# Two batches loaded as nine tokens per partition, both weights ahead of the second batch, and the min/add of two blocks on GpSimd

## The chip, the cores and the metric

The kernel runs on one core of a Trainium2 chip. The time is the device time of that core in microseconds (us). The programs have one core, so a run is called slow when it lies over 1.5% above the fastest run of the same kernel; verdicts use the other ("fast") runs. Every ratio below is the mean time of one kernel's fast runs over the mean time of the fast runs of the kernel before in the same rounds on the same chip, so it is not quite the ratio of the medians that are quoted beside it. One per cent is 4.0 us.

The engines are TensorE (PE in the profile; PEld is its weight load), VectorE (DVE), ScalarE (ACT), GpSimd (POOL), and SyncE (SP), which issues most DMAs. Each has its own queue of instructions.

## The reference, cut to what matters

```python
# per batch (8) and head (8), 576 tokens, 64 wide
out_d = softmax(mean4(q) @ mean4(k).T / 8) @ mean4(v)            # 144 pooled tokens
out_l = softmax(where(|i-j| < 4, q @ k.T / 8, -1e9)) @ v         # a band of 7
x = repeat4(out_d) + out_l                                       # 4608 x 512 in all
h = x @ w_in                                                     # 512 -> 2048
g = where(h > 0, h, exp(min(h, 0)) - 1)                          # ELU
y = g @ w_out                                                    # 2048 -> 512
```

The kernel handles heads in pairs, attention by batch (576 tokens), and the two products in 9 blocks of 512 tokens. "mm1" is x @ w_in, 16 pieces of 4 matmuls a block (tile hp); "mm2" is g @ w_out, 16 pieces as well (tile op).

## The kernel before: the parts that matter

The ELU is max(h,0) + (min(exp(h),1) - 1). In every block ScalarE makes the exp, and VectorE both following steps:

```python
def mm1(t, fc):
    tag = "misc" if t < 2 and fc % 2 else "hp"           # four banks in blocks 0 and 1, two later
    hp = ps.tile([128, TBLK], FP32, tag=tag, bufs=2, name="hp")
    # ... four matmuls into hp
    nc.scalar.activation(out=e[:], in_=hp[:], func=AF.Exp)
    nc.vector.tensor_scalar(                              # "the min/add"
        out=e[:], in0=e[:], scalar1=1.0, scalar2=-1.0, op0=AB.min, op1=AB.add)
    nc.vector.scalar_tensor_tensor(                       # frees the hp bank
        out=gts[t][:, fc, :], in0=hp[:], scalar=0.0, op0=AB.max, in1=e[:], op1=AB.add)
```

q, k and v come with one token per partition, so each run in memory is 64 floats, 256 B; GpSimd casts everything that is loaded (q, k, v, weights) to fp16 and adds the two attention outputs into x:

```python
nc.sync.dma_start(out=q32[:], in_=rows(q, 0, NB, 0, QB))   # [96 tokens][12 blocks][64]
# ... k and v with three DMAs each (edge rows)
nc.gpsimd.tensor_copy(out=q16[:], in_=q32[:].rearrange("p e c d -> p c e d"))   # k, v likewise
```

Weights are loaded in 16 pieces through three buffers, mixed into the loads of batch 1; the softmax denominators of a batch are 36 matmuls (288 or 144 columns).

The softmax here doesn't subtract the row's maximum and nothing guards it: scores larger than these inputs give would overflow.

Of the kernel before, what the change touches and what calls it, by code (L numbers as in the profile page):

```python
# [17 lines left out]
QB, KW, NB = 96, 102, 6  # L18
HB = 3 * QB
QW, KWW = QB + 24, 24 + KW  # L20
# [5 lines left out]
RW = S + SD  # L26
KG = SD // 2


def _np_consts():  # L30

    off = np.concatenate([np.arange(96), np.arange(-3, 0), np.arange(96, 99)])
    m = np.zeros((KW, NB, QB), dtype=np.float16)
    for c in range(NB):
        for u in range(QB):
            ok = (np.abs(off - u) < 4) & (off + QB * c >= 0) & (off + QB * c < S)
            m[ok, c, u] = 1.0
    r = np.zeros((KW, 24), dtype=np.float16)
    r[np.arange(96), np.arange(96) // 4] = 0.25
    qi = np.concatenate([np.eye(96, dtype=np.float16), r[:96]], axis=1)  # L40
    ki = np.concatenate([r, np.eye(KW, dtype=np.float16)], axis=1)
    vr = np.zeros((KW, 120), dtype=np.float16)
    vr[:, 48:72] = r
    indl = np.zeros((128, 37), dtype=np.float16)
    indl[:, 5] = 1.0
    seed = np.zeros((2, 32 + HB), dtype=np.float16)
    seed[0, 6:32] = 1.0
    seed[1, 4:6] = 1.0
    seed[0, 32:] = 1.0
    seed[1, 32 + SD :] = 1.0  # L50
    sel = np.zeros((NPAIR, 32, 3, 2, 64), dtype=np.float16)
    for e in range(2):
        for g in range(2):
            sel[:, 2 * e + g, g, e] = 1.0
        sel[:, 4 + e, 2, e] = 1.0
    return m, qi, ki, vr, indl, seed, sel.reshape(128, 384)
# [12 lines left out]
def kernel(  # L69
# [14 lines left out]

    def const(a, name):
        t = sb.tile(list(a.shape), FP16, tag=name, bufs=1, name=name)
        nc.sync.dma_start(out=t[:], in_=nc.inline_tensor(a, name=name + "c").ap())
        return t

    def two(name):  # L90
        return ps.tile([128, 2, 512], FP32, tag="two", bufs=2, name=name)

    m_np, qi_np, ki_np, vr_np, ind_np, seed_np, sel_np = _np_consts()
    QI, KI = const(qi_np, "QI"), const(ki_np, "KI")
    consts = {}

    def late_consts():
        consts["VR"] = const(vr_np, "VR")
        consts["MASK"] = const(m_np, "MASK")
        consts["IND"] = const(ind_np, "IND")  # L100
        consts["SEED"] = const(seed_np, "SEED")
        consts["SEL"] = const(sel_np, "SEL")
# [4 lines left out]
    def load_weights(i):  # L107

        w32 = sb.tile([128, 1024], FP32, tag="w32", bufs=3, name="w32")
# [9 lines left out]
        return lambda: nc.gpsimd.tensor_copy(out=to, in_=w3)  # L119


    st16, stT, stB, stS, stR = {}, {}, {}, {}, {}

    st32 = {}

    def load(b, j):
        q32 = sb.tile([QB, 2, NB, 64], FP32, tag="q32", bufs=3, name="q32")
        k32 = sb.tile([KW, 2, NB, 64], FP32, tag="k32", bufs=3, name="k32")
        v32 = sb.tile([KW, 2, NB, 64], FP32, tag="v32", bufs=3, name="v32")

        def rows(src, c0, nblk, tok, n):
            a = src[b, 2 * j]
            blocks = [[QB * D, 2 * NB]] if nblk == NB else [[S * D, 2], [QB * D, nblk]]
            return bass.AP(
                tensor=a.tensor, offset=a.offset + (QB * c0 + tok) * D,
                ap=[[D, n], *blocks, [1, D]],
            )

        nc.sync.dma_start(out=q32[:], in_=rows(q, 0, NB, 0, QB))
        for src, dst in ((k, k32), (v, v32)):  # L140
            nc.sync.dma_start(out=dst[0:96], in_=rows(src, 0, NB, 0, QB))
            lo = 1 if (b, j) == (0, 0) else 0
            hi = NB - 1 if (b, j) == (B - 1, NPAIR - 1) else NB
            if lo or hi < NB:
                nc.gpsimd.memset(dst[96:KW, :, 0 if lo else NB - 1, :], 0.0)
            for c0, nblk, tok, p in ((lo, NB - lo, -3, 96), (0, hi, QB, 99)):
                to, a = dst[p : p + 3, :, c0 : c0 + nblk, :], rows(src, c0, nblk, tok, 3)
                if nblk == NB:
                    nc.sync.dma_start(out=to, in_=a)  # L149
                else:  # L150
                    for e in range(2):
                        nc.sync.dma_start(out=to[:, e], in_=a[:, e])
        st32[(b, j)] = (q32, k32, v32)

    def cast(b, j):
        q32, k32, v32 = st32.pop((b, j))
        q16 = sb.tile([QB, NB, 2, 64], FP16, tag="q16", bufs=2, name="q16")
        k16 = sb.tile([KW, NB, 2, 64], FP16, tag="k16", bufs=2, name="k16")
        v16 = sb.tile([KW, NB, 2, 64], FP16, tag="v16", bufs=8, name="v16")
        nc.gpsimd.tensor_copy(out=q16[:], in_=q32[:].rearrange("p e c d -> p c e d"))  # L160
        nc.gpsimd.tensor_copy(out=k16[:], in_=k32[:].rearrange("p e c d -> p c e d"))
        nc.gpsimd.tensor_copy(out=v16[:], in_=v32[:].rearrange("p e c d -> p c e d"))
        st16[(b, j)] = (q16, k16, v16)


    def transposes(b, j):
        q16, k16, v16 = st16.pop((b, j))
        VR = consts["VR"]
        tq, tk = two("tq"), two("tk")
        for c in range(NB):  # L170
            nc.tensor.matmul(  # L171
                tq[:, c // 3, QW * (c % 3) : QW * (c % 3) + QW], q16[:, c, :, :], QI[:],
                start=True, stop=True,
            )
        for c in range(NB):
            nc.tensor.matmul(  # L176
                tq[0:KG, c // 3, 3 * QW : 3 * QW + 128],
                VR[:, 48 - 24 * (c % 3) : 120 - 24 * (c % 3)], v16[:, c, :, :],
                start=(c % 3 == 0), stop=(c % 3 == 2),
            )  # L180
        qt = sb.tile([128, 2, 3 * QW], FP16, tag="qt", bufs=2, name="qt")
        nc.scalar.copy(out=qt[:], in_=tq[:, :, 0 : 3 * QW])  # L182
        vd = sb.tile([KG, 2, 128], FP16, tag="vd", bufs=8, name="vd")
        nc.vector.tensor_copy(out=vd[:], in_=tq[0:KG, :, 3 * QW : 3 * QW + 128])  # L184
        for c in range(NB):
            nc.tensor.matmul(  # L186
                tk[:, c // 3, KWW * (c % 3) : KWW * (c % 3) + KWW], k16[:, c, :, :], KI[:],
                start=True, stop=True,
            )
        tk4 = tk[:, :, 0 : 3 * KWW].rearrange("p g (c w) -> p g c w", w=KWW)  # L190
        kt = sb.tile([128, 2, 3, KW], FP16, tag="kt", bufs=2, name="kt")
        nc.scalar.copy(out=kt[:], in_=tk4[:, :, :, 24:KWW])  # L192
        kd = sb.tile([128, 2, 3, 24], FP16, tag="kd", bufs=2, name="kd")
        nc.vector.tensor_copy(out=kd[:], in_=tk4[:, :, :, 0:24])  # L194
        stT[(b, j)] = (qt, kt, kd, vd, v16)


    def scores(b, j):
        qt, kt, kd, vd, v16 = stT.pop((b, j))
        sc = [two("sc"), two("sc")]  # L200
        for c in range(NB):
            for e in range(2):
# [3 lines left out]
                    kt[r, c // 3, c % 3, :],  # L206
                    qt[r, c // 3, QW * (c % 3) : QW * (c % 3) + QB],
                    start=True, stop=True,
                )
        for kg in range(2):  # L210
            for e in range(2):
                r = slice(64 * e, 64 * e + 64)
                qd = _free(qt[r, 0, QB : QB + 1], [[QW, NB], [1, 24]])
                nc.tensor.matmul(  # L214
                    sc[e][0:KG, kg, HB : HB + SD],
                    _free(kd[r, 0, 0, 0:1], [[1, SD]])[:, KG * kg : KG * kg + KG], qd,
                    start=True, stop=True,
                )
        pex = sb.tile([KW, 2, S], FP16, tag="pex", bufs=2, name="pex")
        dex = sb.tile([KG, 2, 2, SD], FP16, tag="dex", bufs=8, name="dex")  # L220
        for e in range(2):
            nc.scalar.activation(  # L222
                out=pex[:, e, :].rearrange("p (g u) -> p g u", g=2),
                in_=sc[e][0:KW, :, 0:HB], func=AF.Exp, scale=SCALE,
            )
            nc.scalar.activation(  # L226
                out=dex[:, e], in_=sc[e][0:KG, :, HB : HB + SD], func=AF.Exp, scale=SCALE,
            )
        mex = sb.tile([KW, 2, S], FP16, tag="mex", bufs=8, name="mex")
        mk = consts["MASK"][:].rearrange("p c u -> p (c u)")  # L230
        mk2 = bass.AP(tensor=mk.tensor, offset=mk.offset, ap=[list(mk.ap[0]), [0, 2], [1, S]])
        nc.vector.tensor_tensor(out=mex[:], in0=pex[:], in1=mk2, op=AB.mult)  # L232
        stS[(b, j)] = (mex, dex, vd, v16)


    def denominators(b):
        den = ps.tile([128, 512], FP32, tag="misc", bufs=2, name="den")
        SEED, IND = consts["SEED"], consts["IND"]
        for j in range(NPAIR):
            nc.tensor.matmul(  # L240
# [44 lines left out]
    def spread_pe(b, j0):  # L285

        rc, SEL = stR[b], consts["SEL"]
        if j0 == 0:
            stB[b] = sb.tile([128, NPAIR, RW], FP16, tag="rcb", bufs=2, name="rcb")
# [212 lines left out]
```

## Time and profile before

| | before |
|---|---|
| median of 2 runs | 402.4 us (401.56 to 403.25) |
| profiled span, mean granted TensorE clock | 401.8 us, 0.979 |
| TensorE busy | 353.0 us, so 48.8 us idle |
| VectorE, ScalarE, GpSimd busy | 254.4, 203.8, 138.7 us |

Three rows of the page's second part (the span in 40 slices of 10 us; the digits are tenths):

```profile
PE   1465688687986899999999999999899899999996
PEclk9999999968999799999999999999999999999999
GB/s 121 189 253 258 190 215 234 265 126 134 198 139 130 189 176 16 172 231 125 28 195 217 118 78 194 226 64 121 172 79 33 102 53 28 49 29 28 52 54 78
```

TensorE is nearly full from 160 us on. Before that it has holes, and the clock that the throttle grants is below 0.9 in three slices (digits 6, 8 and 7). The first slices move little, 121 and 189 GB/s. The same in the table by stage, for 0 to 10 us and for the stretches of block 0's and of block 1's mm1 (columns: stretch, its length, then busy us and instructions of each engine, granted clock, DMA share, GB/s):

```profile
0.00:10.00 10.00, 1.28 (x12) 1.16 (x13) 0.00 (x0) 1.28 (x1) 3.03 (x9) 1.00 0.67 120
...
45.00:72.00 27.00, 22.21 (x150) 10.80 (x149) 22.40 (x38) 15.03 (x29) 16.04 (x21) 1.00 1.12 224
...
108.00:143.00 35.00, 28.47 (x307) 16.07 (x305) 26.91 (x51) 21.75 (x42) 16.24 (x22) 0.90 0.84 158
```

Three milestones in TensorE's timeline (start, length, engine, line, operation, output<-input, shapes, count): mm1 of block 0, mm2 of block 0 and mm1 of block 1 begin here. Next come the denominators of a later batch, at full clock:

```profile
44.86 0.61 PE L368 MATMUL hp<-xt,WI 128*128 128x512 f16 x1
...
72.49 1.02 PE L388 MATMUL op<-WO,gt 128*128 128x512 f16 x4 [0.83 <-DVE gt L377]
...
108.07 1.03 PE L368 MATMUL hp<-xt,WI 128*128 128x512 f16 x4
...
306.08 0.30 PE L240 MATMUL den<-SEED 2*32 2x288 f16 x4
306.32 0.68 PE L248 MATMUL den<-mex,IND 102*32 102x288 f16 x16
306.82 0.42 PE L257 MATMUL den<-dex,IND 72*32 72x144 f16 x16
307.18 0.60 PE L388 MATMUL op<-WO,gt 128*128 128x512 f16 x2
```

And two groups of the page's fifth part (busy us, mean ns of one | idle time before them, and what ended it):

```profile
L377 DVE SCALAR_TENSOR_TENSOR gt<-hp,e 128x512 f16<-128x512 f32 x144 | 99.6, 692 | 5.4
L374 DVE TENSOR_SCALAR e<-e 128x512 f16<-128x512 f16 x144 | 63.8, 443 | 51.5 <-ACT e L373 50.5
```

The min/add takes 0.443 us on average, and VectorE's last step, 0.692 us, hardly ever waits.

### The profile page before, as it was taken

The numbers are of one execution on the slowest core, as the hardware profiler recorded it, in microseconds if no ns is written. First come the engines' busy times: TensorE is split into PE (matmuls) and PEld (weight loads), VectorE is DVE, ScalarE is ACT, GpSimd is POOL, SyncE is SP. The second block draws the span as 40 slices with busy tenths as digits, with TensorE's granted clock in tenths as the row PEclk, the third lists the DMA queues.
The fourth block names the chain that finished last, engine by engine and source line by source line (L and its number), as shares of the span: only waits on it lengthen the run. The fifth ranks groups of instructions, "written<-read, shape, count | busy, mean of one in ns | idle before, by whom it ended". The sixth has DMA issues, their size and how long they took to land.

```text
span 401.8 us, 8092 instructions
## 1 busy us (share of the span) xinstructions
PE 353.0 (88%) x3052; PEld 185.6 (46%) x3052; DVE 254.4 (63%) x460; ACT 203.8 (51%) x377; POOL 138.7 (35%) x184
## 2 busy tenths in 40 slices
PE   1465688687986899999999999999899899999996
PEld 1352345343553455555545554555454444444442
DVE  0134599732586797697778769886886585555510
ACT  1462157535385376747564855667375334444321
POOL 3365755460850581075028304820450050000000
PEclk9999999968999799999999999999999999999999
DMA  6998999965966980796199639926820310100112
GB/s 121 189 253 258 190 215 234 265 126 134 198 139 130 189 176 16 172 231 125 28 195 217 118 78 194 226 64 121 172 79 33 102 53 28 49 29 28 52 54 78
DMA packets 138082, 53.81 MB, mean 134 GB/s; under 512 B 122580, under 2 KB 131388, under 8 KB 138044
## 3 DMA queue, kind: packets, MB, share of 16 engines
q1 hardware_dynamic: 129420, 47.62, 55.0%
q10 hardware_dynamic: 8624, 5.68, 6.6%
q8 instruction: 24, 0.39, 0.4%
q14 instruction: 14, 0.11, 0.1%
HBM read 43.33 MB, written 9.95 MB: 133 GB/s over the span
## 4 chain that ended last, share of the span: by engine, by line
PE 67%; DMA 12%; POOL 6%; issue 4%; DVE 4%; SPq 3%; ACTq 2%; ACT 1%; POOLq 0%; DVEq 0%
PE op L388 29%; PE hp L368 25%; PE sc L204 2%; PE tk L186 2%; PE tq L176 2%; DVE e L374 2%; PE tq L171 2%; PE lg L325 2%; POOL xt L352 2%; DMA w_170<-in_moe_w_in_dram 2%; DMA rcb<-rd 2%; SPq L149 2%; ACTq L276 2%; DMA w_161<-in_moe_w_in_dram 1%; DMA w_207<-in_moe_w_out_dram 1%
## 5 line engine op out<-in xcount | busy, mean ns | idle before, releaser
L368 PE MATMUL hp<-xt,WI 128*128 128x512 f16 x576 | 150.9, 389 | 4.5 <-DVE gt L377 2.5
L388 PE MATMUL op<-WO,gt 128*128 128x512 f16 x576 | 147.7, 385 | 4.7 <-POOL WO L119 3.8
L373 ACT ACTIVATE e<-hp 128x512 f16<-128x512 f32 x144 | 85.7, 601 | 109.5 <-PE hp L368 90.8
L377 DVE SCALAR_TENSOR_TENSOR gt<-hp,e 128x512 f16<-128x512 f32 x144 | 99.6, 692 | 5.4
L374 DVE TENSOR_SCALAR e<-e 128x512 f16<-128x512 f16 x144 | 63.8, 443 | 51.5 <-ACT e L373 50.5
L368 PEld LDWEIGHTS <-WI 128*128 128x128 f16 x576 | 54.5, 99 | 71.7 <-issue 13.4
L388 PEld LDWEIGHTS <-gt 128*128 128x128 f16 x576 | 54.6, 99 | 68.8 <-issue 7.6
L232 DVE TENSOR_TENSOR mex<-pex,MASK 102x1152 f16<-102x1152 f16 x32 | 29.6, 926 | 40.3 <-ACT pex L222 40.2
L352 POOL TENSOR_TENSOR xt<-ln,gn 128x512 f16<-128x512 f16 (+7 forms) x64 | 42.0, 688 | 34.7 <-DVE ln L343 34.7
L222 ACT ACTIVATE pex<-sc 102x576 f16<-102x576 f32 x64 | 41.4, 647 | 22.3 <-PE sc L214 22.3
L182 ACT CAST qt<-tq 128x720 f16<-128x720 f32 x32 | 24.3, 760 | 30.7 <-PE tq L176 27.3
L394 ACT COPY os<-op 128x512 f32<-128x512 f32 x36 | 21.2, 588 | 25.3 <-PE op L388 25.3
L204 PE MATMUL sc<-qt,kt 64*102 64x96 f16 x384 | 19.1, 226 | 11.5 <-DVE vd L184 6.0
L184 DVE CAST vd<-tq 72x256 f16<-72x256 f32 x32 | 13.2, 413 | 22.3 <-ACT qt L182 22.3
L204 PEld LDWEIGHTS <-kt 64*102 64x102 f16 x384 | 14.4, 135 | 25.8 <-ACT kt L192 12.6
L226 ACT ACTIVATE dex<-sc 72x288 f16<-72x288 f32 x64 | 25.8, 404 | 0.0
L343 DVE TENSOR_TENSOR ln<-lg,rcb 128x576 f16<-128x576 f32 x32 | 23.9, 748 | 0.0
L192 ACT CAST kt<-tk 128x612 f16<-128x612 f32 x32 | 21.8, 680 | 0.1
L176 PEld LDWEIGHTS <-VR 102*72 102x72 f16 x192 | 14.2, 123 | 5.7 <-issue 3.9
L263 DVE RECIPROCAL rc<-den 128x288 f16<-128x288 f32 x8 | 15.6, 1949 | 1.7 <-PE den L257 1.7
L340 DVE TENSOR_TENSOR gn<-lg,rcb 128x144 f16<-128x144 f32 x32 | 9.6, 301 | 5.7 <-POOL xt L352 3.0
L194 DVE CAST kd<-tk 128x144 f16<-128x144 f32 x32 | 9.6, 300 | 1.7 <-ACT kt L192 0.5
(361 smaller groups left out, 265.7 us busy)
## 6 DMA issues: line engine op xcount, KB each, us to landing
out_dram<-os SPq DMA_DIRECT2D x36, 256.0 KB
rcb<-rd ACTq DMA_DIRECT2D x14, 288.0 KB
rcb<-rd ACTq DMA_DIRECT2D x14, 72.0 KB
w_149<-in_moe_w_in_dram SPq DMA_DIRECT2D x1, 512.0 KB
w_152<-in_moe_w_in_dram SPq DMA_DIRECT2D x1, 512.0 KB
w_155<-in_moe_w_in_dram SPq DMA_DIRECT2D x1, 512.0 KB
w_158<-in_moe_w_in_dram SPq DMA_DIRECT2D x1, 512.0 KB
w_161<-in_moe_w_in_dram SPq DMA_DIRECT2D x1, 512.0 KB
```

The source lines that it names most:

```text
L182: nc.scalar.copy(out=qt[:], in_=tq[:, :, 0 : 3 * QW])
L204: nc.tensor.matmul(sc[e][0:KW, c // 3, QB * (c % 3) : QB * (c % 3) + QB], kt[r, c // 3, c % 3, :], qt[r, c // 3, QW * (c % 3) : QW * (c % ...
L222: nc.scalar.activation(out=pex[:, e, :].rearrange("p (g u) -> p g u", g=2), in_=sc[e][0:KW, :, 0:HB], func=AF.Exp, scale=SCALE,)
L226: nc.scalar.activation(out=dex[:, e], in_=sc[e][0:KG, :, HB : HB + SD], func=AF.Exp, scale=SCALE,)
L232: nc.vector.tensor_tensor(out=mex[:], in0=pex[:], in1=mk2, op=AB.mult)
L343: nc.vector.tensor_tensor(out=ln[:].rearrange("p (g u) -> p g u", g=2), in0=lg[:, :, 0:HB], in1=rcb[:, j, 0:S].rearrange("p (g u) -> p g u ...
L352: nc.gpsimd.tensor_tensor(out=xt(t)[:, j, t0 - TBLK * t : t1 - TBLK * t], in0=ln[:, a:z], in1=_rep4(gn[:, a // 4 : z // 4]), op=AB.add,)
L368: nc.tensor.matmul(hp[:], WI[:, dc, 128 * fc : 128 * fc + 128], x[:, dc, :], start=(dc == 0), stop=(dc == DMC - 1),)
L373: nc.scalar.activation(out=e[:], in_=hp[:], func=AF.Exp)
L374: nc.vector.tensor_scalar(out=e[:], in0=e[:], scalar1=1.0, scalar2=-1.0, op0=AB.min, op1=AB.add)
L377: nc.vector.scalar_tensor_tensor(out=gts[t][:, fc, :], in0=hp[:], scalar=0.0, op0=AB.max, in1=e[:], op1=AB.add)
L388: nc.tensor.matmul(op_[:], gts[t][:, fc, 128 * tt : 128 * tt + 128], WO[:, fc, :], start=(fc == 0), stop=(fc == FCN - 1),)
```

## The change

The intent: batches 0 and 1 load q and k as nine consecutive tokens per partition (2.3 KB runs instead of 256 B). 64 x 64 transposes leave the tokens out of order, and the copies out of PSUM put them right by reading with a stride. Both weights are loaded before batch 1. Then mm1 of block 0 runs without attention beside it, and mm2 of block 0 runs beside batch 1's attention. v takes one DMA a pair. Denominators are 96 matmuls of 72 columns in place of 36 wider ones, with a smaller reciprocal. Six of the 16 weight casts move to ScalarE, and the hp products of block 1 get two PSUM banks in place of four. The min/add of blocks 0 and 1 moves to GpSimd.

```diff
+            if nines(b):                         # b < 2
+                ap = [[LR * D, 2 * LP], [1, LR * D]]        # 128 runs of 576 floats
...
+    def copy_nines(to, tp, copy):
+        copy(out=to.rearrange("p (t r) -> p t r", r=LR),
+             in_=t2.rearrange("p (r t) -> p t r", r=LR))
...
+    def add_fours(b, j):                         # sums of four tokens, on VectorE
+        nc.vector.tensor_reduce(...)             # q and k
...
-        tag = "misc" if t < 2 and fc % 2 else "hp"
+        hp = bank("misc" if t == 0 and fc % 2 else "hp", "hp")
...
-        nc.vector.tensor_scalar(
+        (nc.gpsimd if t < 2 else nc.vector).tensor_scalar(
             out=e[:], in0=e[:], scalar1=1.0, scalar2=-1.0, op0=AB.min, op1=AB.add
         )
...
+    for s in range(16):
+        at(T1 + s, mm1, 0, s)                    # block 0 alone
+    for j in range(NPAIR):                       # then batch 1, with mm2 of block 0 between
+        at(T2 + 4 * j, early_turn, 1, j, nc.scalar.copy)
...
+        if b == 2:
+            for j in range(3):
+                at(-20 + j, load_qk, b, j)       # batch 2's loads: after mm2 of block 0
+                at(-20 + j, load_v, b, j)
```

## The prediction

> **What bounds the kernel now.** From 160 us on, TensorE: in the table by stage it is busy 39.9 of every 40 us (160 to 280 us). Before that it is not: it is busy for 117.6 of 160 us, so 42 of the kernel's 49 idle us lie there, and the granted clock falls to 0.78 (80 to 100 us) and 0.83 (120 to 140 us). In the first 80 us the DMA share is 0.87 to 1.19 at only 155 to 256 GB/s: 122,580 of 138,082 packets are under 512 B. The Trainium skill ("DMA: Bandwidth & Descriptors", Specifications) asks for at least 512 B for line rate; q and k come in 256 B runs, and the first q tile (288 KB) takes 3.9 us from issue to cast. Milestones in TensorE's timeline: mm1 of block 0 starts at 44.9 us (steadily at 48.6), mm2 of block 0 at 72.5 (and stops 3.8 us for a w_out cast), mm1 of block 1 at 108.1.
>
> **What changes.**
> - Loads: about 15.7 MB (batches 0 and 1, all weights) are needed in both; 4.7 MB of them (q, k) move from 256 B to 2.3 KB runs. Estimate: batch 0's q and k landed by 10 us.
> - Batch 0: 36 small transposing matmuls a pair; ACT copy (about 0.65), DVE copy (0.75), two DVE sums (about 0.65 each). ACT has 2.75 us a pair (exps 0.647 and 0.404, twice), the cycle is about 4 us against 5.2 to 8.3 now. Scores end near 25 us (now 31.5); mm1 of block 0 starts near 36.
> - mm1 of block 0: 13.8 us of matmul, but GpSimd now does the min/add (about 0.65 each, 16 of them), eight w casts at 1.04 and the adds: about 18 us. Ends near 55.
> - Batch 1 beside mm2 of block 0: a chain of about 5.5 us a pair (two double banks), then sums, denominators, four ends: about 30 us. mm1 of block 1 starts near 87.
> - Block 1: GpSimd has 16 min/adds beside 2.7 us of casts a pair; with two hp banks, some 5 us of stalls.
> - Every batch: denominators become 96 matmuls of 72 columns instead of 36 of 144 to 288 (1.15 us now). Estimate +0.8 us each, +5 us in the TensorE-bound part. The reciprocal shrinks from 1.95 to about 0.5 us, there off the critical path.
> - The rest (steady part, last 14.7 us of mm2 alone) is unchanged.
>
> **Sum.** At 108.1 us the kernel before has also done about 5.4 us of batch 2's TensorE work, so its comparable point is 102.5; after's is 87: 15.5 us gained. Denominators give back 5. Waits and slow clock after this point cost about 9.5 us now, some 6 afterwards: 3 gained. 402.4 - 15.5 + 5 - 3 = 389.
>
> **Prediction:** 389 us, 8 in 10 between 380 and 398. Faster by over 2%: 0.76; within 2%: 0.21; slower: 0.03.
>
> **What would show each step.** TensorE timeline: first hp matmul at 34 to 39 us; first op at 56 to 60; mm1 of block 1 at 83 to 91. Table by stage: TensorE still full in the last 230 us. Groups: tq of 64 columns, den at about 2 us a batch, reciprocal near 0.5 us; a GpSimd group of 32 min/adds.
>
> **What would make it wrong.** Strided PSUM reads well over 0.7 us a copy; GpSimd's min/add at 1 us or more (its 512-column add takes 1.06), stretching blocks 0 and 1 by 5 to 10 us; small matmuls limited by issue (740 more, 20 ns each would be 15 us); the clock staying low. Better than predicted: if the 42 idle us shrink below 25.

## The result, and the profile after

| | before | after |
|---|---|---|
| median of 2 runs | 402.4 us | 442.23 us (440.26 to 444.2) |
| ratio, 95% interval | | 1.1007 (1.0861 to 1.1152) |
| profiled span, mean granted clock | 401.8 us, 0.979 | 438.5 us, 0.914 |
| TensorE busy, idle (span less busy) | 353.0, 48.8 us | 368.7, 69.8 us |
| GpSimd busy | 138.7 us | 190.2 us |

The kernel became 10% slower; 389 us (380 to 398) had been expected. The same three rows of the page (a slice is now 11 us):

```profile
PE   4866464977556478998999999999999999999996
PEclk9968965978588875899999999999999999999999
GB/s 279 235 358 381 125 94 31 49 28 48 196 193 186 112 91 178 50 118 201 126 167 141 194 110 150 163 93 167 94 26 25 46 97 25 49 24 49 49 48 72
```

The loads are much better: 279 GB/s in the first slice, 358 and 381 in the third and fourth, and then little for 60 us. But TensorE is busy for only 109 of the first 171 us: 62 of its 70 idle us lie there. The table by stage shows where:

```profile
0.00:10.00 10.00, 3.92 (x91) 3.46 (x92) 3.35 (x5) 4.24 (x7) 4.00 (x17) 1.00 0.85 279
...
30.00:66.00 36.00, 20.96 (x64) 7.09 (x64) 9.61 (x16) 13.59 (x20) 35.62 (x29) 0.82 0.66 213
66.00:72.00 6.00, 0.00 (x0) 0.00 (x0) 2.43 (x4) 0.60 (x1) 6.00 (x4) 0.57 0.00 0
...
112.00:171.00 59.00, 37.37 (x365) 22.28 (x366) 17.74 (x33) 26.03 (x49) 45.40 (x36) 0.73 1.02 155
```

From 30 to 66 us, mm1 of block 0, GpSimd is busy for 35.62 of 36 us (16.04 of 27 before), and it stays full until TensorE can go on at 72 us. From 112 to 171 us, mm1 of block 1, it has 45.40 of 59 us. The milestones, and the denominators at full clock:

```profile
30.07 1.01 PE L508 MATMUL hp<-xt,WI 128*128 128x512 f16 x2
...
73.44 3.60 PE L528 MATMUL op<-WO,gt 128*128 128x512 f16 x8
...
116.57 3.62 PE L508 MATMUL hp<-xt,WI 128*128 128x512 f16 x8
...
230.60 0.45 PE L384 MATMUL den<-mex,IND 112*32 112x72 f16 x32
230.87 0.31 PE L384 MATMUL den<-dex,IND 72*32 72x72 f16 x16
231.00 0.43 PE L384 MATMUL den<-mex,IND 112*32 112x72 f16 x32
231.26 0.31 PE L384 MATMUL den<-dex,IND 72*32 72x72 f16 x16
231.50 1.04 PE L528 MATMUL op<-WO,gt 128*128 128x512 f16 x4
```

mm1 of block 0 starts 15 us earlier than before. By mm2 of block 0 that lead is gone, and block 1 starts 8.5 us late. The denominators, which were expected to cost more, cost less (230.60 to 231.50, 0.90 us, against 306.08 to 307.18, 1.10 us). The groups by line:

```profile
L517 DVE SCALAR_TENSOR_TENSOR gt<-hp,e 128x512 f16<-128x512 f32 x144 | 99.6, 691 | 70.9 <-POOL e L514 66.3
L514 DVE TENSOR_SCALAR e<-e 128x512 f16<-128x512 f16 x112 | 43.6, 390 | 45.6 <-ACT e L513 44.1
L514 POOL TENSOR_SCALAR e<-e 128x512 f16<-128x512 f16 x32 | 62.1, 1955 | 9.5 <-ACT e L513 9.5
```

A min/add on GpSimd takes 1.955 us on average (29 of the 32 take 1.91 to 1.92 us, three take 2.00 to 2.53). VectorE's last step, which frees the hp bank, now waits 66.3 us for it. In the list of TensorE's waits this arrives as its largest entry:

```profile
PE hp L508 <- DVE gt L517: 26.6, 19, 2.6
...
PE tq L242 <- POOL q L211: 6.4, 1, 6.4
...
PE tq L233 <- POOL q L214: 5.0, 1, 5.0
```

(us in total, times, longest. The two others are the waits for the cast of batch 1's and of batch 2's first q.) GpSimd's own timeline in block 0 shows the queue. Three min/adds take 5.68 us, then a cast follows, and so on to the end of the block. Since mm1 delivers a piece every 0.86 us, GpSimd sets the pace:

```profile
36.43 5.68 POOL L514 TENSOR_SCALAR e<-e 128x512 f16<-128x512 f16 x3
42.06 1.04 POOL L157 CAST WO<-w 128x1024 f16<-128x1024 f32 x1
```

The theory (A) was therefore that these 32 instructions, three times as long as predicted, are the loss. The rivals were: GpSimd is overloaded by casts and adds anyway (B); the low clock is a cause of its own (also B); the new schedule, not the instruction, makes it hurt (C).

### The profile page after: what moved, and what is told of

Read it like the earlier page. It is cut to its first block, busy times and chain, and to the rows that moved or that the text cites. A ratio compares the mean times of both kernels' runs of the same rounds, so it can differ in the third digit from the quotient of the medians.

```text
span 438.5 us, 9325 instructions
## 1 busy us (share of the span) xinstructions
PE 368.7 (84%) x3792; PEld 195.9 (45%) x3792; DVE 233.5 (53%) x436; ACT 210.6 (48%) x395; POOL 190.2 (43%) x214
## 4 chain that ended last, share of the span: by engine, by line
PE 59%; POOL 8%; issue 6%; DMA 5%; ACT 3%; DVE 1%; ACTq 1%; SPq 0%; POOLq 0%
PE op L528 27%; PE hp L508 20%; POOL e L514 5%; DMA rd<-rc 2%; PE lg L448 2%; PE sc L321 2%; DMA v<-in_v_dram 2%; PE tq L233 1%; PE tq L295 1%; PE tk L233 1%; PE den L384 1%; DMA k<-in_k_dram 1%; POOL v L221 1%; ACT pex L343 1%; POOL q L214 1%
## 5 line engine op out<-in xcount | busy, mean ns | idle before, releaser
L517 DVE SCALAR_TENSOR_TENSOR gt<-hp,e 128x512 f16<-128x512 f32 x144 | 99.6, 691 | 70.9 <-POOL e L514 66.3
L475 POOL TENSOR_TENSOR xt<-ln,gn 128x64 f16<-128x64 f16 (+7 forms) x64 | 42.0, 686 | 114.5 <-DVE ln L468 114.5
L514 DVE TENSOR_SCALAR e<-e 128x512 f16<-128x512 f16 x112 | 43.6, 390 | 45.6 <-ACT e L513 44.1
L514 POOL TENSOR_SCALAR e<-e 128x512 f16<-128x512 f16 x32 | 62.1, 1955 | 9.5 <-ACT e L513 9.5
L343 ACT ACTIVATE pex<-sc 112x576 f16<-112x576 f32 x64 | 40.9, 646 | 18.0 <-PE sc L331 13.9
L358 DVE TENSOR_TENSOR mex<-pex,MASK 112x1152 f16<-112x1152 f16 x32 | 26.4, 826 | 25.1 <-ACT pex L343 24.9
L214 POOL CAST q<-q 96x768 f16<-96x768 f32 x24 | 19.9, 830 | 29.9 <-issue 22.5
L221 POOL CAST v<-v 112x768 f16<-112x768 f32 x32 | 28.5, 895 | 7.0 <-DMA v<-in_v_dram 7.0
L321 PEld LDWEIGHTS <-kt 64*112 64x112 f16 x384 | 15.1, 143 | 19.6 <-issue 8.0
L321 PE MATMUL sc<-qt,kt 64*112 64x96 f16 x384 | 19.3, 233 | 5.4 <-ACT dex L349 1.3
L214 POOL CAST k<-k 96x768 f16<-96x768 f32 x24 | 20.1, 839 | 1.5 <-DMA k<-in_k_dram 1.5
```

Of the source, the lines that this page charges most:

```text
L214: nc.gpsimd.tensor_copy(out=t, in_=x.rearrange("p (e c d) -> p c e d", e=2, d=D))
L221: nc.gpsimd.tensor_copy(out=t[:], in_=st32.pop(("v", b, j)).rearrange("p (e c) d -> p c e d", e=2))
L321: nc.tensor.matmul(sc[e][0:KW, c // 3, QB * (c % 3) : QB * (c % 3) + QB], kt[r, QB * c : QB * c + KW], q_of(b, j, r, c), start=True, stop= ...
L343: nc.scalar.activation(out=stS[(b, j)][2][:, e, :].rearrange("p (g u) -> p g u", g=2), in_=sc[e][0:KW, :, 0:HB], func=AF.Exp, scale=SCALE,)
L358: nc.vector.tensor_tensor(out=mex[:], in0=pex[:], in1=mk2, op=AB.mult)
L475: nc.gpsimd.tensor_tensor(out=xt(t)[:, j, t0 - TBLK * t : t1 - TBLK * t], in0=ln[:, a:z], in1=_rep4(gn[:, a // 4 : z // 4]), op=AB.add,)
```

## The experiments

Twelve kernels ran. Each is the changed kernel with the edit shown, unless the text says otherwise.

### e1 to e3: the min/add back on VectorE, in both blocks or in one

```diff
-        (nc.gpsimd if t < 2 else nc.vector).tensor_scalar(
+        nc.vector.tensor_scalar(                              # e1
+        (nc.gpsimd if t == 0 else nc.vector).tensor_scalar(   # e2
+        (nc.gpsimd if t == 1 else nc.vector).tensor_scalar(   # e3
```

> The changed kernel with the min/add of blocks 0 and 1 back on VectorE; nothing else differs. Theory A (the 1.92 us GpSimd min/add paces blocks 0 and 1): mm1 of block 0 takes about 18 us instead of 36 (VectorE then has 16 x 1.13), the 6.4 us wait for the batch-1 q cast mostly goes, block 1 takes about 33 us instead of 60; total about 390 us (383 to 398), and the low granted clock in the first 180 us goes with the waits. Rival B (GpSimd is full with casts and adds anyway, or the low clock is a cause of its own): still over 425 us. The 5 us hole before batch 2's first transpose stays in both.

> Only block 0's min/add on GpSimd. Theory A: mm1 of block 0 takes 36 us as in the changed kernel, block 1 as in the run with all on VectorE: about 22 us slower than that run, so about 412 us. Rival B: no difference to the run with all on VectorE.

> Only block 1's min/add on GpSimd. Theory A: block 1 takes about 60 us, about 27 us slower than the run with all on VectorE, so about 417 us; the costs of the two blocks add up to the whole distance between the changed kernel and the run with all on VectorE. If the clock were one common cause, they would not add.

Measured: e1 398.69 us, ratio 0.9835 (0.9767 to 0.9902); e2 421.31 us, 1.0397 (1.0328 to 1.0465); e3 418.21 us, 1.0322 (1.0254 to 1.0389). So one word had cost 11.7% of the kernel before's time. Block 0's part is 5.6% (about 23 us, as expected), block 1's is 4.9% (20 us, where 27 were expected). Their sum, 10.5%, agrees with the whole within the intervals. Rival B falls. GpSimd is no longer full during mm1 of block 0, which takes 20 us in e1 (18 expected):

```profile
30.00:51.00 21.00, 17.68 (x74) 6.59 (x72) 17.72 (x31) 13.56 (x22) 14.48 (x19) 1.00 1.09 351
```

e1 is faster than before (1.65%; by the interval a gain of 2% is neither shown nor excluded), but its total lies just above the range, and block 1 takes 38 us (93.29 to 130.99), not 33. Something else was still wrong.

### e4: only this instruction moved, in the kernel before

```diff
-        nc.vector.tensor_scalar(            # kernel before
+        (nc.gpsimd if t < 2 else nc.vector).tensor_scalar(
```

> The kernel before with nothing changed but the min/add of blocks 0 and 1 moved to GpSimd. Theory A: GpSimd gets 61 us of work in stretches (45 to 72 us and 108 to 142 us) where it was 30 to 65% busy: 30 to 50 us slower than before, about 440 us. Rival C (only the new schedule with its two hp banks and casts in front makes it hurt): under 415 us.

Measured: 443.46 us, ratio 1.0974 (1.0901 to 1.1047). The old schedule loses nearly as much from this one word as the new one does (9.7% against 11.7%). Rival C falls.

### e5: what the GpSimd instruction costs, by form

Eight forms in turn over the pieces of blocks 0 and 1:

```diff
+ fc % 8:  0 min 1.0, add -1.0 (512 columns)   1 min alone      2 add alone
+          3 the first on 256 columns          4 on 128         5 tensor_copy
+          6 mult 1.0, add -1.0                7 tensor_tensor e + e
```

> Wrong result on purpose, one look: the changed kernel with eight forms of the GpSimd instruction in turn in blocks 0 and 1 (four of each): two-op min/add on 512, 256 and 128 columns, min alone, add alone, mult/add, a plain copy, a tensor-tensor add. Theory A1 (time goes by element, and the two-op form is a slow loop): two-op 1.92, about 1.0 and 0.55 us at 512, 256 and 128 columns, single ops well below 1 us, copy about 0.55 us. Rival A2 (min is what is slow): min alone as slow as min/add, mult/add fast. Rival A3 (a fixed cost[...]): the 128-column form over 1 us too.

Measured (groups by line of this run; the lines stand in the order two-op min/add, add alone, min alone, 256 columns, e + e, 128 columns, mult/add, copy):

```profile
L517 POOL TENSOR_SCALAR e<-e 128x512 f16<-128x512 f16 x4 | 7.7, 1921 | 1.5 <-ACT e L513 1.5
...
L521 POOL TENSOR_SCALAR e<-e 128x512 f16<-128x512 f16 x4 | 6.1, 1526 | 1.1 <-ACT e L513 1.1
L519 POOL TENSOR_SCALAR e<-e 128x512 f16<-128x512 f16 x4 | 6.0, 1488 | 0.0
...
L523 POOL TENSOR_SCALAR e<-e 128x256 f16<-128x256 f16 x4 | 4.3, 1077 | 5.6 <-ACT e L513 5.6
...
L531 POOL TENSOR_TENSOR e<-e 128x512 f16<-128x512 f16 x4 | 4.1, 1037 | 0.6 <-ACT e L513 0.6
L525 POOL TENSOR_SCALAR e<-e 128x128 f16<-128x128 f16 x4 | 2.5, 638 | 0.0
L529 POOL TENSOR_SCALAR e<-e 128x512 f16<-128x512 f16 x4 | 2.5, 619 | 1.9 <-ACT e L513 1.9
L527 POOL COPY e<-e 128x512 f16<-128x512 f16 x4 | 2.4, 611 | 2.2 <-ACT e L513 2.2
```

The time goes by the element: from 128 to 512 columns it grows by 1921 - 638 = 1283 ns, 3.3 ns an element (of one partition), and little is fixed: 638 less 128 such elements leaves about 0.2 us. That rules out A3. Min alone is not special: add alone takes as long (1.49 and 1.53 us), so A2 falls too, although its fast mult/add came true, and so does A1's guess that single operations are quick. What is quick is the copy (0.61 us) and multiply-then-add (0.62 us). Two instructions with the same name and shape differ by a factor of 3.1 in the operations that they name. Why that is so inside GpSimd no run here shows.

This is the figure that the prediction got wrong. The prediction does not say where its 0.65 us comes from; GpSimd's casts run at about such a rate (1024 columns in 1.04 us). The Trainium skill ("GPSIMD Engine Reference", section 4.1, Engine selection) says the same of the class: instructions with one input are "roughly line-rate". The copy and the multiply-add agree with that; min/add, min and add do not, and here the measurement decides.

### e9: the prediction's assumption made true

```diff
-            out=e[:], in0=e[:], scalar1=1.0, scalar2=-1.0, op0=AB.min, op1=AB.add
+            out=e[:], in0=e[:], scalar1=1.0, scalar2=-1.0,
+            op0=AB.mult if t < 2 else AB.min, op1=AB.add,
```

> Wrong result on purpose: the changed kernel as it is, GpSimd instruction and all, but in blocks 0 and 1 it computes e*1-1 (mult/add, 0.62 us in the run with eight forms) instead of min(e,1)-1 (1.92 us). This is what the prediction had assumed (0.65 us). Theory A1 (only the size of that instruction was wrong; where it runs was not): mm1 of block 0 takes about 17 us instead of 36, block 1 about 35 us, total 392 us (388 to 398), no slower than the run with all on VectorE (398.7), since VectorE is relieved of it. Rival: moving the work to GpSimd hurts by its place too (queue behind casts[...]): over 403 us.

Measured: 403.89 us, ratio 1.0010 (0.9954 to 1.0065). Its output is wrong, which doesn't matter for the time. The instruction's length alone is thus worth 1.1007 - 1.0010, 10.0% or about 40 us. But the run is not as fast as e1: its ratio is 1.75% (about 7 us) above, against what I expected of A1 and on the rival's side. The place costs something even at 0.62 us. The group by line, and what stands in GpSimd's timeline in block 1:

```profile
L514 POOL TENSOR_SCALAR e<-e 128x512 f16<-128x512 f16 x32 | 19.5, 621 | 17.8 <-ACT e L513 17.2 <-DMA v<-in_v_dram 0.4
...
104.95 0.82 POOL L214 CAST q<-q 96x768 f16<-96x768 f32 x1
105.71 0.82 POOL L214 CAST k<-k 96x768 f16<-96x768 f32 x1
106.49 0.82 POOL L221 CAST v<-v 112x768 f16<-112x768 f32 x1
107.28 1.20 POOL L514 TENSOR_SCALAR e<-e 128x512 f16<-128x512 f16 x2
```

Three casts of 0.82 us stand in front of the next min/adds in the queue. TensorE's waits on a bank (hp after VectorE's last step) are 8.4 us here and 4.1 us in e1. In block 0 the same queue works the other way round: batch 1's first casts come behind the last min/add, and TensorE waits 2.0 us for the first of them (in e1 not for q, and 0.6 us for a k). Of the 6.9 us between the two profiled runs, 0.7 lie before the first hp matmul, where the edit is not yet at work, 2.7 between that and mm2 of block 0, 0.8 in the batch-1 stage and 3.2 in block 1; 0.5 came back later. That the queue is the cause is read from these traces; no run reordered it at 0.62 us.

### e6 and e8: batch 2's loads and casts earlier

In e1 TensorE still waits 5.1 us for the cast of batch 2's first q, and 2.4 us for its v. The changed kernel shows the reason in SyncE's timeline: the loads stand behind the last output store of mm2 of block 0, which waits for its data.

```profile
106.73 0.33 SPq L536 DMA_DIRECT2D out_dram<-os  x1
107.17 0.43 SPq L175 DMA_DIRECT2D q<-in_q_dram  x1
```

Both edits are on e1; e8 has both:

```diff
-                at(-20 + j, load_qk, b, j)             # e6 (load_v likewise)
+                at(T2 + 8 + 0.1 * j, load_qk, b, j)
...
-  (slots[2 * j - 2] if j else -3.1 if b > 2 else -1)   # e8: when batch 2's first casts are queued
+  (slots[2 * j - 2] if j else -3.1 if b > 2 else T2 + 13)
```

> All min/adds on VectorE, and batch 2's first three pairs of loads issued 8 steps into the batch-1 stage instead of behind mm2 of block 0's last output store in the SyncE queue. Theory D (the 5.1 and 2.4 us that TensorE waits for the casts of batch 2's first q and v is a queue-order hole): both waits shrink to under 2.5 us in sum (the adds on GpSimd still stand in front of the cast), total about 5 us under the run with all on VectorE, about 393.5 us. Rival: GpSimd's adds set the time of that cast, and less than 2 us is gained.

> As the run with early loads, and batch 2's first casts put in front of batch 1's adds in GpSimd's queue. Theory D: TensorE finds q of batch 2 ready, the hole after batch 1's last spread is gone (under 1 us), total about 392 us. If the adds did not matter: equal to the run with early loads.

Measured: e6 395.47 us, ratio 0.9807 (0.9754 to 0.9859), which the intervals do not separate from e1's 0.9835. The wait for v shrank from 2.4 to 0.8 us, the wait for q stayed at 5.0 us. So the rival was right about q. In GpSimd's timeline of e6 the adds of batch 1 stand in front of the cast, with no gap:

```profile
84.31 2.40 POOL L475 TENSOR_TENSOR xt<-ln,gn 128x448 f16<-128x448 f16 x5 [0.94 <-DVE ln L468]
86.65 0.82 POOL L214 CAST q<-q 96x768 f16<-96x768 f32 x1
```

e8 reorders just that: 387.76 us, ratio 0.9616 (0.9561 to 0.9672). TensorE's timeline has the last spread of batch 1 (rb: matmuls that copy the reciprocals to the rows of each head) and the first transpose of batch 2 back to back:

```profile
84.39 0.49 PE L420 MATMUL rb<-rc,SEL 32*128 32x72 f16 x10
84.81 0.49 PE L233 MATMUL tq<-I,q 96*128 96x120 f16 x6
...
86.98 1.94 PE L508 MATMUL hp<-xt,WI 128*128 128x512 f16 x8
```

mm1 of block 1 starts at 86.98 us, where the prediction had it (87). The two queue orders, SyncE's and GpSimd's, are together worth 2.2% (about 9 us). Moving the loads alone did not close the hole for q; moving the casts alone was not tried. e8 is also 4 us faster than expected: against e6, its block 1 takes 35 us instead of 39 (86.98 to 122.13 against 90.25 to 129.23), and why was not tested. e8 beats the kernel before by 3.8%.

### e7: the long runs undone

On e1, q and k of batches 0 and 1 go back to 256 B runs and blocks of 96:

```diff
     def nines(b):
-        return b < 2
+        return False
...
-        copy_nines(qt[:, 0:S], tq, nc.scalar.copy)      # and k, and add_fours
+        copy_q(b, j, tq, nc.scalar.copy)
+        copy_k_blocks(b, j, tk, copy_k, nc.vector.tensor_copy)
```

> All min/adds on VectorE, but q and k of batches 0 and 1 loaded in 256 B runs and turned in blocks of 96 as in the other batches: the title's first part undone. By rates of the first 10 us (120 GB/s before, 268 with 2.3 KB runs) batch 0's q and k land some 8 us later, while two 0.74 us sums a pair go away from VectorE: first hp matmul at about 36 us instead of 30.5, total about 404 us, 5 us over the run with all on VectorE. If the long runs are worth nothing: within 1.5 us of it.

Measured: 403.18 us, ratio 1.0004 (0.9955 to 1.0053), 1.7% (7 us) over e1; the first hp matmul is at 34.7 us (e1: 30.45 us). The profiled runs differ by 4.4 us, most of it in that start. The first 10 us of this run move 185 GB/s by its table by stage, against 268 in e1. (The kernel before, also with 256 B runs, moved 120, so the run length is not all of the gain over it.) The Trainium skill ("DMA: Bandwidth & Descriptors", Specifications) asks for at least 512 B for line rate, and this agrees in direction; it has runs of 256 B and 2.3 KB and nothing between. The edit also undoes the transposes and sums that go with the long runs, so it sizes the two together. So the part that the change is named for is a real gain, and without it the rest of the change, on VectorE, only equals the kernel before.

### e10, e11, e12: three attempts to go on from e8

```diff
-  10.5), 11.2, (17, 18)          # e10: batch 2's denominators later
+  10.5), 12.6, (17, 18)
...
-        nc.vector.tensor_scalar(  # e11: every fourth min/add of block 0 on GpSimd
+        (nc.gpsimd if t == 0 and fc % 4 == 3 else nc.vector).tensor_scalar(
...
-  bank("misc" if t == 0 and fc % 2 else "hp", "hp")   # e12: four banks for block 1 too
+  bank("misc" if t < 2 and fc % 2 else "hp", "hp")
```

> The run with early loads and casts (387.8 us), with batch 2's denominators 1.4 steps later. TensorE waits 2.3 us there for the last masked scores; if that wait is real cost, it goes and the total falls by 1 to 2 us to about 386.5; if the outputs of batch 2 then wait for the spread reciprocals instead, nothing is gained.

> The run with early loads and casts (387.8 us), with every fourth min/add of block 0 on GpSimd. VectorE is what limits mm1 of block 0 there (16 x (0.69 + 0.28 to 1.14) us). If the engines worked independently, it would win about 2 us (386). In the run with all on VectorE its min/add took 0.28 us alone and 1.0 to 1.1 us when a GpSimd cast ran beside it; theory E, that GpSimd work delays VectorE's two-operation instruction, expects nothing gained or 1 to 4 us lost (388 to 392), and VectorE's min/adds near 2 us beside those of GpSimd.

> The run with early loads and casts (ratio 0.962 to the kernel before), with block 1's hidden products alternating over four banks as in the kernel before (the change had left two for block 1). There TensorE waits 5.8 us for a free bank (VectorE's last step), 1.5 us at a time. If two banks are the limit in block 1, about 3 us are gained (ratio about 0.954, 384 us); if VectorE's throughput is the limit, or the bank is then missing for the denominators, under 1 us.

e10, a miss: 391.77 us, ratio 0.9709 (0.964 to 0.9778), slower if anything. The 2.3 us wait is down to 0.4, and a wait of 4.4 us has come for batch 2's outputs (the matmuls lg wait for VectorE's ln, the scaling of the outputs, which needs the spread reciprocals).

e11: 393.33 us, ratio 0.9745 (0.9694 to 0.9797), about 5 us slower than e8. The direction was expected, the reason was not: VectorE's min/adds between those of GpSimd took 0.28 to 0.64 us, not near 2. VectorE's min/add can be slower beside GpSimd: in e1 it took 0.28 us at 48.02 us, with GpSimd idle, and 1.12 us at 35.92 us, inside a row of GpSimd casts from 32.84 to 36.89 us. What the trace of e11 suggests instead is the queue again. GpSimd's last min/add starts at 54.08 us, and the first cast of batch 1's q behind it at 55.99 us; in e8 that cast starts at 45.30 us. (This profile fell on a slow run, so I use its order, not its total; the cause is not tested on its own.)

e12: 388.64 us, ratio 0.9584 (0.9557 to 0.9612), which the intervals do not separate from e8. The bank waits fell from 5.8 to 1.9 us, but waits for VectorE's vd (its copy of the pooled v, 2.5 us) and ln (1.9 us) stand in their place. So VectorE, not the banks, seems to limit block 1, which was not tested on its own. Whether e12 is better than e8 stays open.

## Why the prediction was wrong

The forecast was 389 us with 0.76 for a gain; the result was 442 us, outside the range.

- **The step that failed** is "GpSimd now does the min/add (about 0.65 each, 16 of them) ... about 18 us. Ends near 55." The instruction took 1.92 us, so block 0's mm1 took 36 us and ended at 66. The same error sits in "Block 1: ... some 5 us of stalls": that stage took 59 us. e9 sizes the length alone: about 40 of the 53 us between forecast and result. The prediction did list "GpSimd's min/add at 1 us or more" among what could go wrong, but gave it only 5 to 10 us.
- **What it had not seen**: even a short instruction costs about 7 us more on GpSimd than on VectorE (e9 against e1), by the traces because a step that TensorE waits for then stands behind casts. And batch 2's loads and casts were queued behind stores and adds, about 9 us (e1 against e8). The three parts add up to 40 + 7 + 9 = 56 us, but only because they are three legs of one way, from the changed kernel over e9 and e1 to e8.
- **Partly luck**: that e8, with the three removed, lands at 388 us, where the sum gave 389, does not prove the sum. In e8 the min/add is on VectorE, not where the forecast had it, and errors cancel: mm1 of block 0 starts 5 us earlier than forecast (30.91 against 36), but takes 21 us instead of 18, and batch 1 takes 33 instead of 30, so that block 1 starts at 86.98 us as forecast. From there the denominators cost about 6 us less than forecast, and still the rest took 301 us where the sum had 302: about as much was lost elsewhere, and the runs do not size where.
- **Batch 0**: better than said. Predicted cycle 4 us a pair, measured 3.1 (score matmuls start at 6.80, 9.69, 12.80 and 15.96 us); first hp matmul at 30.07 us against "near 36". The strided PSUM reads, feared, take 0.64 us on ScalarE.
- **Denominators**: wrong sign. Predicted +0.8 us a batch, measured -0.2 (0.90 against 1.10 us at full clock; this holds for the four batches of the changed kernel that ran at it). The 96 matmuls go out at 0.90 / 96 = 9.4 ns each, weight loads included. The fear that small matmuls are limited by issue did not come true in this group.
- **Batch 1 beside mm2 of block 0**: predicted 30 us; e8 has 33 (52 to 85 us).
- **The reciprocal**: about 0.5 us predicted, 0.60 measured. The steady part is full as predicted (259.5 of 267 us from 171 us on).
- **The low clock** (0.57 in the empty 6 us, 0.73 to 0.82 in the two slow stages) goes with the waits. The Trainium skill ("TensorE: Matmul & The Clock Gate", Part 1) says that the default clock is throttled and activity releases it. The 0.57 while TensorE stood still agrees, and with the same schedule but the min/add on VectorE the mean rose from 0.914 to 0.974. How many of the 40 us are the clock and how many the waits themselves was not separated.

## What to carry to other kernels

Before moving an elementwise step to another engine, time that very form there: the same instruction name at the same shape took 0.62 or 1.92 us by its two operations, and no cast or add in the trace would have told (1.04 us for a cast of 1024 columns, 1.06 for an add of 512). Be wary of putting a step that frees a PSUM bank into one queue with bulk casts, even when the engine has room on average: here it cost about 7 us. And read each queue, DMA-issuing ones too, at the seams between stages: a load issued behind a store that waits, and a cast behind adds, made a hole that moving the loads alone did not close.

## What the Trainium skill lacked or had wrong

- "GPSIMD Engine Reference", section 4.1 (Engine selection), calls instructions with one input roughly line-rate. For 128 x 512 fp16 that holds for a copy (0.61 us) and mult/add (0.62 us), not for min (1.49 us), add (1.53 us) or min/add (1.92 us; 1.08 at 256 and 0.64 at 128 columns). The page has a measured time for a tensor_tensor add (section 3.1), but none of a tensor_scalar by its operations.
- "TensorE: Matmul & The Clock Gate", Part 1, states that start-to-start never drops below about 25 ns however small the matmul. 96 matmuls of 72 columns that cycle through four column positions took 0.90 us, 9.4 ns each with their weight loads, so their starts lie under 10 ns apart on average. Part 3 of the page, on packing small matmuls, does describe such overlap.
